# A planner that schedules backward and forward in turn, in a clustered attention with two dense layers

## The chip, the cores and the metric

The kernel runs on one core of a Trainium2 chip. The metric is the device time of one execution in microseconds. The kernel before took 800.88 us (median of three runs, 799.55 to 801.35).

## The reference

Inputs are q, k and v of shape (2, 8, 768, 64), sixteen centroids for each of the 8 heads, and two dense layers with weights 512x2048 and 2048x512 each. A query sees a key only if both have the same nearest centroid:

```python
mask = q_assign[:, :, :, None] == k_assign[:, :, None, :]
scores = np.where(mask, scale * np.matmul(q, k.transpose(0, 1, 3, 2)), -1000000000.0)
attn = softmax(scores)                 # over the keys
x = np.matmul(attn, v)                 # -> (1536, 512), heads side by side
h = x @ w_in;  x = (h * sigmoid(h)) @ w_out
h = x @ w2_in; x = (max(h, 0) + alpha * min(h, 0)) @ w2_out
```

All inputs and the output are float32.

## The kernel before

**Tiles and stages.** The 1536 tokens are 12 tiles of 128. Attention goes in 96 units, one for each tile and head. Every float32 operand is split into a high and a low float16 part, so that a product takes three float16 matmuls (high-high, high-low, low-high).

A unit has a front and a back. `front(u)` runs four matmuls of 384 columns into a score bank (lines 765 and 769; there are two such banks, so two units can be between scores and softmax), a row minimum on VectorE (779), the exponential on ScalarE (784), the high part on ScalarE (791) and the low part on VectorE (793). `front_t(u)` issues one DMA that transposes the unit's probabilities (799). `back(u)` runs eighteen matmuls of 64 columns with v (811); it comes two units behind its front in the program. When the eight heads of a tile are done, line 837 normalizes the tile, and its transposed halves (line 842) are what the first layer reads.

The four weight matrices come in eight pieces each (line 865). A piece is reassembled from its bits on ScalarE (876, 880) and VectorE (887, 890), its sum of squares is taken with eight matmuls (921) and one VectorE instruction (923), and it is split into high and low (902 on ScalarE, 903 on VectorE). The output weights of a layer are split only when all their eight sums are known. `layer1(c)` works through seven chunks of one or two tiles: matmuls of 128 or 256 columns into the w banks (1150), four elementwise instructions (1157, 1158, 1161, 1162), and matmuls with the output weights (1181). `layer2(j)` does the same in three parts of 512 columns (1252, then 1261 to 1266, then 1283). The raw pieces of the second layer's weights lie where attention had its keys and values, so they are loaded from the end of attention on. The sums of squares of the first layer's weights and the chunks' products take the same two w banks in turn, in program order.

**What sets the order.** Each engine and the SP queue of DMAs work in order. The program is first written in one sequence by Python generators (fixed constants say how many units of attention go beside each chunk). At the end `plan_order` hands all instructions to `Plan`, which simulates the engines: `costs` (lines 73 to 107) prices each instruction by its size, `data_deps` (144 to 176) finds which instruction must follow which from the memory cells they touch, and `run(prio)` (178 to 281) is a list scheduler: whenever an engine is free, it takes the ready instruction with the smallest `prio`. The order that comes out is then forced on each engine with order-only dependencies. The priorities are the places in the program:

```python
end, order = plan.run(list(range(len(plan.ins))))
```

Three of its prices are used below. A VectorE instruction of n elements costs 0.145 + n/955 us (0.06 more with a scalar operand from memory), a ScalarE one 0.19 + n/1205 us, and a DMA transposition of n elements per partition lands 1.3 + n/750 + 0.33 us after its issue when the queue is free. In `run`, all DMAs go one behind the other through one `queue`. A PSUM operand is found by `in_psum`, and `cells` gave one cell for each bank of it.

Of the kernel before, what the change touches and what calls it, by code (L numbers as in the profile page):

```python
# [2 lines left out]

# [35 lines left out]
EXP_ON = ("aaaaaaaa", "aaaaaaaa", "aaaaaaaa", "aaaaaaaa")  # L39
P_LO_DVE = range(96)  # L40

MASK = 2.0 ** 15
BIT23 = 2.0 ** 23


class Plan:
# [78 lines left out]
    def cells(self, a):  # L125
        import numpy as np

        b = a.bass_ap
        name = b.tensor.name.rsplit("_", 1)[0]
        if type(b.tensor).__name__.startswith("DRam"):  # L130
            return None, None
        it = 2 if a.dtype in (F16, BF16) else 4
        dims = [list(x) for x in a.ap]
        at = np.array([b.offset % dims[0][0]], dtype=np.int64)
        for st, c in dims[1:]:
            if st:
                at = (at[:, None] + np.arange(c) * st).ravel()
        cell = np.unique(at * it // 4)
        if self.in_psum(a):
            return "ps" + name, np.unique(cell // 512)  # L140
        return name, cell

    def data_deps(self):
# [4 lines left out]
        for n, i in enumerate(self.ins):  # L148
# [26 lines left out]
            found.discard(n)  # L175
            self.deps[n] = sorted(found)

    def run(self, prio):
        import heapq

        N, ne = len(self.ins), len(self.ENGINES)
# [10 lines left out]
        now, later = [[] for _ in range(ne)], [[] for _ in range(ne)]  # L192
        order = [[] for _ in range(ne)]
        queue = end = 0.0
        port = [0.0] * ne
        other = {1: 3, 3: 1}
        window = [0, False, 0.0]
# [4 lines left out]
        for _ in range(N):  # L202
            while True:
                best = None
                for e in range(ne):
                    while later[e] and later[e][0][0] <= free[e]:
                        t, p, n = heapq.heappop(later[e])
# [4 lines left out]
                    t = free[e] if now[e] else later[e][0][0] if later[e] else None  # L212
                    if t is not None and (best is None or t < best[0]):
                        best = (t, e)
                t, e = best
# [3 lines left out]
                p, n = now[e][0]  # L219
# [14 lines left out]
            n = heapq.heappop(now[e])[1]  # L234
            for x in held:
                heapq.heappush(now[e], x)
            s, c = free[e], self.cost[n]
            kind = self.ENGINES[e]
            if kind == "PE":
# [7 lines left out]
                t = c[0] if window[1] else 1.6 * c[0]  # L247
                free[e] = busy[e] = s + t
                done = s + t + 0.23
# [14 lines left out]
            elif kind == "SP":  # L264
# [3 lines left out]
                done = own = queue + 0.33  # L268
                flight.append([done, b, s, n])
            else:  # L270
# [2 lines left out]
                    port[e] = s + c[0] - 0.13  # L273
                done = own = s + c[0] + 0.06
            end = max(end, done)
            order[e].append(n)
            for m, only in after[n]:
                at = s if only else own if self.eng[m] == e else done
# [7 lines left out]
def plan_order(tc, nc, starts):  # L286
    plan = Plan(list(nc.cur_bb.bb.instructions))
    place = {i.name: n for n, i in enumerate(plan.ins)}
    for a, b in starts:
        plan.order_only[place[a]].append(place[b])  # L290
    end, order = plan.run(list(range(len(plan.ins))))
    for line in order:
        for a, b in zip(line, line[1:]):
            tc.add_manual_dep(
                plan.ins[b], plan.ins[a].name,
                mybir.DependencyInfo(mybir.DependencyClass.NoSync, mybir.DependencyReason.DATA),
                reason="planned order",
            )
    return end
# [3 lines left out]
def cluster_attention_silu_prelu(  # L303
# [230 lines left out]
    def one_hot(sims, n, w2, o, a, b, en):  # L534


        y = view(o + KB, F16, n, C)
        z = view(o, F16, n, C)
        m = scr(n)
        nc.vector.reduce_max(out=m, in_=sims, axis=AX.X)  # L540
        nc.vector.tensor_tensor(out=y, in0=sims, in1=bc(m, C), op=ALU.is_equal)
        nc.vector.tensor_tensor(
            out=z, in0=y, in1=rev.unsqueeze(1).to_broadcast([128, n, C]), op=ALU.mult
        )
        m2 = scr(n // 2).bitcast(F16)
        nc.vector.reduce_max(out=m2, in_=z, axis=AX.X)
        nc.vector.tensor_tensor(out=y, in0=z, in1=bc(m2, C), op=ALU.is_equal)
        en.tensor_scalar(w2[:, :, D:D + C], y, a, b, op0=ALU.mult, op1=ALU.add)
# [9 lines left out]
    def k_pre(b, pr):  # L558
        return o_x2 + 6 * KB * pr if b == 0 else o_x2 + (8 + 6 * (pr % 2)) * KB
# [83 lines left out]
    def prep_k_b(b, pr):  # L643
# [4 lines left out]
        for g in range(G):  # L648
            h = 2 * pr + g // T
            for i, c in enumerate((0, 2)):  # L650
# [3 lines left out]
                )  # L654
        one_hot(sims, G, w2, k_pre(b, pr), -MASK, MASK, nc.gpsimd if b or pr else nc.vector)
        k_t2[b, pr] = nc.sync.dma_start_transpose(
# [3 lines left out]
        for j in range(2):  # L660
# [5 lines left out]
        nc.vector.tensor_scalar(  # L666
            has[D:D + C, b, 2 * pr:2 * pr + 2], missing[D:D + C], MASK * (S - 0.5), None,
            op0=ALU.is_lt,
# [38 lines left out]
    def prep_q_b(n):  # L707
# [3 lines left out]
        for h in range(H):  # L711
            for i in range(2):
# [3 lines left out]
                )  # L716
        one_hot(sims, H, w2, o_preq, -MASK, 0.0, nc.gpsimd if n else nc.vector)
        q_t2[n] = nc.sync.dma_start_transpose(
# [4 lines left out]
    def head_scales(n, pairs):  # L723
# [4 lines left out]
        if pairs[0] == 0:  # L728
            (nc.gpsimd if n else nc.vector).tensor_scalar(
                d, isk[b], q_inv[:, n % 2:n % 2 + 1], 1.0 / float(D) ** 0.5 / MASK,  # L730
                op0=ALU.mult, op1=ALU.mult,
# [615 lines left out]
    for j in range(NC2):  # L1347
        layer2(j)
    plan_order(tc, nc, starts)


# [30 lines left out]
```

## Time and profile before

| what | value |
|---|---|
| median of 3 runs | 800.88 us (799.55 to 801.35) |
| the profiled execution | 802.03 us |
| its span, first to last instruction | 800.2 us |
| mean granted TensorE clock | 0.968 of full speed |
| TensorE matmuls busy | 704.5 us, 88% of the span |
| VectorE busy | 539.4 us, 67% |
| ScalarE busy | 450.1 us, 56% |
| GpSimd busy | 144.0 us, 18% |
| DMA queue q1, share of the 16 engines | 59.7% |

PE is TensorE's matmuls, PEld its weight loads (which run beside matmuls), DVE is VectorE, ACT ScalarE, POOL GpSimd, SP the queue that issues all DMAs. A mean over the span says little here, since the kernel goes through stages; the rows below are by stage.

### The profile page before, as it was taken

The page shows a single profiled execution, that of the slowest core. Times are in us where ns is not written, and L with a number is a line of the kernel's source. Part 1 is how long each engine was busy: PE and PEld are TensorE (multiplying, and loading weights), DVE is VectorE, ACT ScalarE, POOL GpSimd, SP SyncE. Part 2 cuts the span into 40 slices and gives each one's busy share as a digit, 9 for nine tenths or more (in the row PEclk, how much of TensorE's full clock was granted, in tenths as well). Part 3 has the DMA queues.
Part 4 walks back from the last instruction along what each step waited for, and adds up shares of the span by engine and source line. Part 5 has one row for each costly group of instructions (what it writes and reads, how often), then busy time and mean ns, then how long its engine had stood idle before and what let it go on. Part 6 is the DMA issues. An engine that isn't in the chain of part 4 may idle for free.

```text
span 800.2 us, 16777 instructions
## 1 busy us (share of the span) xinstructions
PE 704.5 (88%) x6932; PEld 497.1 (62%) x6932; DVE 539.4 (67%) x1024; ACT 450.1 (56%) x725; POOL 144.0 (18%) x237
## 2 busy tenths in 40 slices
PE   1446657779999999999999989999899999999998
PEld 1344445658888887888877879785444444444443
DVE  5589998887678689759867777969940286017700
ACT  7957777777678667758746776866430132012200
POOL 4642131122512643213211030000000000000000
PEclk9996659999999999999999999999999999999999
DMA  9969998879998998997897967630000000000000
GB/s 271 263 169 250 283 279 136 142 152 144 169 171 149 165 173 146 144 171 136 144 130 114 286 172 198 235 135 1 0 1 27 26 1 1 27 26 1 1 27 26
DMA packets 241596, 101.89 MB, mean 127 GB/s; under 512 B 217328, under 2 KB 227568, under 8 KB 241392
## 3 DMA queue, kind: packets, MB, share of 16 engines
q1 hardware_dynamic: 241520, 100.83, 59.7%
q8 instruction: 54, 0.88, 0.5%
q14 instruction: 22, 0.18, 0.1%
HBM read 44.08 MB, written 3.15 MB: 59 GB/s over the span
## 4 chain that ended last, share of the span: by engine, by line
PE 54%; DMA 9%; DVE 5%; issue 3%; ACT 3%; POOL 2%; SPq 0%; POOLq 0%; ACTq 0%
PE w L1283 10%; PE w L1252 9%; PE w L1150 8%; DMA arena<-arena 7%; PE w L1181 7%; PE m L1283 5%; PE m L1252 4%; PE x L811 3%; PE s L765 2%; DMA arena<-in_moe_w_out_dram 2%; PE s L769 1%; DVE arena L903 1%; PE s L921 1%; PE m L1150 1%; DVE arena L890 1%
## 5 line engine op out<-in xcount | busy, mean ns | idle before, releaser
L1181 PE MATMUL w<-arena 128*128 128x256 f16 (+1 forms) x1248 | 132.6, 256 | 5.0 <-ACT arena L1161 2.1
L1150 PE MATMUL w<-arena 128*128 128x256 f16 (+1 forms) x1200 | 127.4, 255 | 2.9 <-DVE arena L1158 1.6
L1181 PEld LDWEIGHTS <-arena 128*128 128x128 f16 x1344 | 114.1, 99 | 18.4 <-DVE arena L903 3.3
L1150 PEld LDWEIGHTS <-arena 128*128 128x128 f16 x1344 | 114.3, 98 | 17.6 <-issue 3.5
L793 DVE TENSOR_TENSOR arena<-arena 128x768 f16<-128x768 f32 x96 | 96.2, 1002 | 26.8 <-ACT arena L791 26.2
L779 DVE TENSOR_SCALAR_CACHE_REDUCE s<-s,stat 128x768 f32<-128x768 f32 x96 | 97.8, 1021 | 16.8 <-PE s L769 10.4
L784 ACT ACTIVATE arena<-s,stat 128x768 f32<-128x768 f32 x96 | 86.0, 896 | 38.8 <-DVE arena L793 26.3
L1252 PEld LDWEIGHTS <-arena 128*128 128x128 f16 x576 | 56.5, 98 | 70.2 <-issue 3.1
L1283 PEld LDWEIGHTS <-arena 128*128 128x128 f16 x576 | 56.3, 98 | 68.0
L791 ACT ACTIVATE arena<-arena 128x768 f16<-128x768 f32 x96 | 80.5, 839 | 24.1 <-DMA arena<-arena 23.7
L1252 PE MATMUL w<-arena 128*128 128x512 f16 x384 | 86.0, 379 | 1.0 <-DVE arena L1262 1.0
L1283 PE MATMUL w<-arena 128*128 128x512 f16 x384 | 83.7, 379 | 0.0
L1261 DVE TENSOR_SCALAR arena<-w,stat 128x512 f32<-128x512 f32 x32 | 23.8, 748 | 88.8 <-PE w L1252 88.8
L1265 ACT ACTIVATE arena<-arena,stat 128x512 f16<-128x512 f32 x48 | 34.3, 720 | 84.2 <-DVE arena L1262 82.3
L765 PE MATMUL s<-arena 80*128 80x384 f16 x192 | 67.9, 354 | 14.7 <-ACT arena L784 9.5
L811 PEld LDWEIGHTS <-arena 128*128 128x128 f16 x1728 | 66.0, 102 | 22.9 <-DMA arena<-arena 17.0
L811 PE MATMUL x<-arena 128*128 128x64 f16 x1728 | 71.3, 199 | 8.9 <-DMA arena<-arena 8.9
L423 POOL TENSOR_SCALAR stat<-stat 128x1 int32<-128x1 int32 x49 | 14.4, 293 | 339.0 <-DVE stat L418 237.3
L769 PE MATMUL s<-arena 128*128 128x384 f16 x192 | 68.2, 355 | 0.0
L1289 ACT ACTIVATE arena<-w,stat 128x512 f32<-128x512 f32 x8 | 5.5, 687 | 73.1 <-PE w L1283 73.1
L903 DVE SCALAR_TENSOR_TENSOR arena<-arena,stat 128x1024 f16<-128x1024 f32 x32 | 41.6, 1311 | 7.1 <-ACT arena L902 7.0
L887 DVE SCALAR_TENSOR_TENSOR arena<-arena 128x1024 int32<-128x1024 int32 x32 | 39.8, 1245 | 9.4 <-ACT arena L880 9.4
(149 smaller groups left out, 1034.1 us busy)
## 6 DMA issues: line engine op xcount, KB each, us to landing
arena<-in_moe_w_in_dram SPq DMA_DIRECT2D x16, 1024.0 KB, 6.2
arena<-in_moe_w_out_dram SPq DMA_DIRECT2D x16, 1024.0 KB, 6.1
arena<-in_k_dram SPq DMA_DIRECT2D x8, 384.0 KB, 4.9
arena<-in_q_dram SPq DMA_DIRECT2D x6, 512.0 KB, 4.5
arena<-in_v_dram SPq DMA_DIRECT2D x8, 384.0 KB, 6.0
out_dram<-arena SPq DMA_DIRECT2D x12, 256.0 KB, 2.0
arena<-arena SPq DMA_TRANSPOSE x149, 4.2
arena<-in_moe_alpha_dram SPq DMA_DIRECT2D x1, 1024.0 KB, 6.6
```

The source lines that it names most:

```text
L765: nc.tensor.matmul(out=sc[:, j, :hs], lhsT=qt2[0:D + C, h], rhs=kt2[0:D + C, h % 2, j * hs:(j + 1) * hs], start=True, stop=False,)
L769: nc.tensor.matmul(out=sc[:, j, :hs], lhsT=qt1[:, h], rhs=kt1[:, h % 2, j * hs:(j + 1) * hs], start=False, stop=True,)
L779: nc.vector.tensor_scalar(sc[:, :, :hs], sc[:, :, :hs], nd_cols[:, H * (n % 2) + h:H * (n % 2) + h + 1], None, op0=ALU.mult, op1=ALU.min, ...
L784: nc.scalar.activation(out=view(o, F32, 2, hs), in_=sc[:, :, :hs], func=ACTF.Exp, scale=-1.0, bias=bias, accum_out=sums[n % 2][:, h:h + 1],)
L791: nc.scalar.activation(out=hl[:, 0], in_=p, func=ACTF.Copy)
L793: en.tensor_tensor(out=hl[:, 1], in0=p, in1=hl[:, 0], op=ALU.subtract)
L811: nc.tensor.matmul(out=x_ps[0][:, h], lhsT=pt[:, ph * T + t], rhs=vt[:, h % 2, t, vh], start=(i == 0), stop=(i == 3 * T - 1),)
L903: nc.vector.scalar_tensor_tensor(out=lo, in0=t, scalar=s, in1=hi, op0=ALU.mult, op1=ALU.subtract)
L1150: nc.tensor.matmul(out=hp[:, ff], lhsT=wi[:, a, kd, ff * 128:ff * 128 + 128], rhs=mov(bb, kd), start=(i == 0), stop=(i == 3 * KD - 1),)
L1181: nc.tensor.matmul(out=acc, lhsT=wo[:, a, f % 2, dt * 128:(dt + 1) * 128], rhs=g[:, f, bb], start=(i == 0), stop=(i == 3 * KF - 1),)
L1252: nc.tensor.matmul(out=hp, lhsT=in_piece(o_a + 24 * KB, f // 2)[:, a, kd, f % 2 * 128:][:, :128], rhs=x[bb][:, kd], start=(i == 0), stop=( ...
L1283: nc.tensor.matmul(out=acc, lhsT=g[:, f, a, t * 128:(t + 1) * 128], rhs=out_piece(o_w, f // 2)[:, bb, f % 2], start=(i == 0), stop=(i == 3 ...
```

## The change

The planner now runs the list scheduler many times. `mirror` makes a copy of the plan with every dependency turned round. `improve` starts with the plan of before (priorities by place in the program). Then sixty times it schedules the mirrored plan with what ended last first, and schedules the real plan again with what ended last in the mirrored one first (those are the instructions with the longest tail of work behind them); a normal noise of 0.1 us is added to the priorities. It keeps the plan with the smallest simulated end, the first one among them. `run` notes when each instruction began and ended. And `cells` gives one cell for a whole PSUM tile: the two halves of a score tile count as one place.

```diff
+PLAN_ROUNDS = 60
...
         if self.in_psum(a):
-            return "ps" + name, np.unique(cell // 512)
+            return "ps" + name, np.zeros(1, np.int64)
         return name, cell
...
+    def mirror(self):
+
+        back = copy(self)
+        back.deps = [[] for _ in self.ins]
+        back.order_only = [[] for _ in self.ins]
+        for n in range(len(self.ins)):
+            for d in self.deps[n]:
+                back.deps[d].append(n)
+            for d in self.order_only[n]:
+                back.order_only[d].append(n)
+        return back
+
+    def improve(self, rounds):
+
+        noise = Random(1)
+        best = self.run(list(range(len(self.ins))))
+        back = self.mirror()
+        for _ in range(rounds):
+            back.run([noise.gauss(0, 0.1) - t for t in self.ended])
+            best = min(best, self.run([noise.gauss(0, 0.1) - t for t in back.ended]), key=lambda x: x[0])
+        return best
+
     def run(self, prio):
...
         queue = end = 0.0
+        self.begun, self.ended = [0.0] * N, [0.0] * N
...
             end = max(end, done)
+            self.begun[n], self.ended[n] = s, done
             order[e].append(n)
...
-    end, order = plan.run(list(range(len(plan.ins))))
+    end, order = plan.improve(PLAN_ROUNDS)
     for line in order:
```

No instruction is added or removed and no buffer is moved; only the order on the five in-order queues can change.

## Rows read from the trace of the kernel before

**Rows 1.** The page, parts 1 and 2: busy time, and tenths in 40 slices of 20 us.

```profile
PE 704.5 (88%) x6932; PEld 497.1 (62%) x6932; DVE 539.4 (67%) x1024; ACT 450.1 (56%) x725; POOL 144.0 (18%) x237
...
PE   1446657779999999999999989999899999999998
...
PEclk9996659999999999999999999999999999999999
```

**Rows 2.** Windows by stage: stretch, length, then busy PE, PEld, DVE, ACT, POOL, clock, DMA, GB/s.

```profile
40.00:123.60 83.60, 50.00 (x519) 36.71 (x516) 78.85 (x163) 58.68 (x80) 23.31 (x34) 0.71 0.97 241
123.60:180.00 56.40, 43.58 (x712) 36.25 (x712) 47.10 (x90) 42.64 (x76) 11.89 (x21) 0.97 0.79 142
180.00:440.00 260.00, 251.56 (x3463) 214.52 (x3462) 197.96 (x405) 180.96 (x330) 75.99 (x102) 1.00 0.91 150
440.00:543.00 103.00, 95.83 (x964) 84.66 (x963) 79.98 (x133) 75.02 (x104) 9.72 (x22) 1.00 0.67 200
543.00:600.00 57.00, 54.26 (x257) 25.06 (x255) 46.25 (x67) 26.63 (x40) 0.34 (x2) 1.00 0.00 1
```

**Rows 3.** Timeline, TensorE (last row ScalarE): start, length, instruction, [idle before].

```profile
123.62 0.27 PE L1150 MATMUL w<-arena 128*128 128x128 f16 x2 [1.12 <-DVE arena L923]
123.73 0.33 PE L765 MATMUL s<-arena 80*128 80x384 f16 x1
...
124.23 0.33 PE L769 MATMUL s<-arena 128*128 128x384 f16 x1
...
478.03 5.95 PE L1181 MATMUL w<-arena 128*128 128x256 f16 x53
...
542.95 0.38 PE L1252 MATMUL m<-arena 128*128 128x512 f16 x1
...
796.49 0.69 ACT L1289 ACTIVATE arena<-w,stat 128x512 f32<-128x512 f32 x1 [9.67 <-PE w L1283]
```

**Rows 4.** Groups of VectorE instructions from 40 to 123.6 us: count | busy, mean ns.

```profile
L887 DVE SCALAR_TENSOR_TENSOR arena<-arena 128x1024 int32<-128x1024 int32 x13 | 16.6, 1276 | 0.0
L890 DVE SCALAR_TENSOR_TENSOR arena<-arena 128x1024 int32<-128x1024 int32 x13 | 16.4, 1260 | 0.0
L779 DVE TENSOR_SCALAR_CACHE_REDUCE s<-s,stat 128x768 f32<-128x768 f32 x16 | 16.2, 1021 | 0.7 <-PE s L769 0.7
L793 DVE TENSOR_TENSOR arena<-arena 128x768 f16<-128x768 f32 x13 | 12.3, 949 | 0.2 <-ACT arena L791 0.2
...
L779 DVE DVE_READ_ACCUMULATOR s<-s,stat 128x1 f32 x16 | 2.2, 136 | 0.0
```

**Rows 5.** Timeline of VectorE: the last splits of weights, the first and last tile's end.

```profile
93.13 1.28 DVE L903 SCALAR_TENSOR_TENSOR arena<-arena,stat 128x1024 f16<-128x1024 f32 x1
...
103.24 0.68 DVE L837 TENSOR_TENSOR arena<-x,stat 128x512 f32<-128x512 f32 x1
...
165.47 2.48 DVE L903 SCALAR_TENSOR_TENSOR arena<-arena,stat 128x1024 f16<-128x1024 f32 x2
...
475.05 0.69 DVE L837 TENSOR_TENSOR arena<-x,stat 128x512 f32<-128x512 f32 x1
```

**Rows 6.** Waits of TensorE from 123.6 to 180 us: total, times, longest.

```profile
PE s L765 <- ACT arena L784: 5.0, 4, 1.7
PE x L811 <- DMA arena<-arena: 2.9, 5, 0.9
...
PE w L1181 <- DVE arena L903: 1.8, 5, 0.7
```

**Rows 7.** The page, part 5: groups over the whole span.

```profile
L1181 PEld LDWEIGHTS <-arena 128*128 128x128 f16 x1344 | 114.1, 99 | 18.4 <-DVE arena L903 3.3
...
L793 DVE TENSOR_TENSOR arena<-arena 128x768 f16<-128x768 f32 x96 | 96.2, 1002 | 26.8 <-ACT arena L791 26.2
...
L791 ACT ACTIVATE arena<-arena 128x768 f16<-128x768 f32 x96 | 80.5, 839 | 24.1 <-DMA arena<-arena 23.7
...
L903 DVE SCALAR_TENSOR_TENSOR arena<-arena,stat 128x1024 f16<-128x1024 f32 x32 | 41.6, 1311 | 7.1 <-ACT arena L902 7.0
```

**Rows 8.** The 96 transpositions of line 799, in ns, and their landing.

```profile
L799 SPq EVENT_SEMAPHORE  x128: 17/28/4110, 39.8 to 464.6; - x128
L799 SPq DMA_TRANSPOSE arena<-arena x96: 1274/1442/5193, 45.4 to 465.0; - x96
...
DMA to landing us min/median/max: 3.6/4.2/9.0
```

**Rows 9.** Waits over the whole span: total us, times, longest.

```profile
PE x L811 <- DMA arena<-arena: 8.9, 16, 1.3
```

More of the change, by code (lines that the diff above doesn't have):

```diff
@@ L2 @@
 from contextlib import ExitStack
+from copy import copy
+from random import Random
 import concourse.bass as bass
```

## The prediction

> **What bounds the kernel now.** I read the page's busy rows first: TensorE is the busiest engine with 704.5 of 800.2 us, and in the 40 slices it is full from the ninth or tenth slice on, while the slices before show tenths of 1 to 7 and, from 60 to 120 us, a granted clock of 0.5 to 0.6, which is mostly the lower of its two levels (1.2 of 2.4 GHz) [rows 1]. So a new order can only win where TensorE has holes, and the second thing to read is a cut of the span at the events that close a stage.
>
> The timeline of TensorE gives the cuts. The first product of the first layer starts at 123.62 us, released by line 923; the second layer starts at 542.95 us; the last eviction begins at 796.49 us, when TensorE is done [rows 3]. Windows between these cuts give TensorE's holes [rows 2]: 83.6 - 50.0 = 33.6 us from 40 to 123.6 us, 56.4 - 43.58 = 12.8 us up to 180, 260 - 251.56 = 8.4 us up to 440, 103 - 95.83 = 7.2 us up to the second layer, 2.7 us in its first 57 us. Behind that TensorE has none, so the 200 us from 600 us on cannot be shortened by any order.
>
> In the first of these windows TensorE is not the bound. VectorE is busy 78.85 of 83.6 us there, 94% [rows 2]. What it does is two sorts of work mixed: pieces of weights (lines 887 and 890 thirteen times each, 33.0 us) and attention (line 779 sixteen times, 793 thirteen times, with the accumulator reads 16.2 + 12.3 + 2.2 = 30.7 us) [rows 4]. The first product needs tile 0, which is eight units; it ended at 103.24 us [rows 5]. The other eight of the sixteen units are tile 1, which the first chunk does not need.
>
> **The change, part by part.** *The sixty rounds.* They add no instruction. What they can alter is which ready instruction an engine takes. The new priority is the length of the tail behind an instruction; weights of the first layer have nearly the whole kernel behind them, tile 1's attention has less. So I expect VectorE and ScalarE to do pieces of weights first and tile 1 later. What that is worth at most: eight times line 779 with its read, 8 x (1.021 + 0.136) = 9.3 us, and five of line 793 beyond tile 0's eight, 5 x 0.949 = 4.7 us, 14.0 us of a full VectorE ahead of 123.62 us [rows 4]. Not all is won: TensorE must then run these eight fronts later, when it is full. Four score matmuls start at intervals of (124.23 - 123.73) / 3 = 0.167 us, so a front is 0.67 us and eight are 5.3 us [rows 3]. Net 14.0 - 5.3 = 8.7 us; since tile 0 itself still has to pass through tile normalization at 103.24 us and its transposition, I take 8. The bounds are 0 and 14.
>
> The moved work lands on VectorE between 180 and 440 us, which has 260 - 197.96 = 62 us free there [rows 2]: that covers the 14 us. If that cover were gone, the same 14 us would come back as holes before 440 us.
>
> *From 123.6 to 180 us*, holes of 12.8 us. TensorE waits 5.0 us for a score bank held by the exponential, 2.9 us for transposed probabilities, 1.8 us for splits of the output weights, which end only at 165.47 + 2.48 us [rows 5, 6]. These splits have a long tail behind them and will be taken earlier; the other two waits can be filled with products if these are ready. Bounds 0 and 12.8, I take half, 6.
>
> *From 180 to 440 us*, holes of 8.4 us, many and small; bounds 0 and 8.4, I take 2. Here a rule of the Trainium skill would say otherwise, so the row comes first. A row of 53 products of 256 columns lasts 5.95 us, and by the 0.27 us that one or two take, the interval is about (5.95 - 0.27) / 52 = 0.109 us [rows 3]; 256 columns at 2.4 GHz would be 0.107. A busy TensorE is thus at its rate here and its holes are all that can be won. The Trainium skill (Perfetto Trace Analysis, Identifying the Most-Contended Engine) says that busy matmul time is a poor measure of the distance to the limit, and that the busy share of weight loads is a good one. By that rule this stretch would have 260 - 214.52 = 45.5 us of room [rows 2], and with a quarter of it the term would be 11 us, not 2. The interval of the products speaks against it, and I stay with the holes.
>
> *From 440 to 600 us*, holes of 7.2 + 2.7 = 9.9 us. VectorE is busy 79.98 of 103 and 46.25 of 57 us there [rows 2], converting the second layer's weights behind the end of attention at 475.05 us [rows 5]. Bounds 0 and 9.9, I take 4.
>
> *The SP queue and the DMAs* are reordered too. A transposition that waits for its unit at the head of the queue holds all DMAs behind it; the waits on line 799 have a median of 0.028 us and a largest of 4.1 us [rows 8]. The change could spare or add such waits; between -4 and +4 us I take 0 and leave the rest to a rival. GpSimd's queue is busy 18% [rows 1]; a step that moves on it has idle time to hide in.
>
> *One cell for a PSUM tile* joins the two halves of a score tile in one chain of four matmuls. Line 779 reads both halves anyway, and the four run in a row in 0.67 us [rows 3]; I cost it at nothing, covered by that. Without the cover it could hold a second half back by one front, 0.67 us now and then.
>
> *Sum.* 8 + 6 + 2 + 4 = 20 us. The profiled execution took 802.0 us, so 782.0 us; it lay 1.15 us above the median of 800.88 us, so **781 us**. A measurement of this kernel can tell about 0.2% from no change.
>
> **Can the planner's prices be trusted?** This decides whether a plan that is shorter in the planner is shorter on the chip. For line 793 it has 0.145 + 768/955 = 0.949 us, the row has 1.002; for line 903 0.145 + 1024/955 + 0.06 = 1.277 against 1.311; for line 791 0.19 + 768/1205 = 0.827 against 0.839 [rows 7]. These are low by 1 to 6%. For a transposition of 1536 elements it has 1.3 + 2.05 + 0.33 = 3.68 us from issue to landing, the row has a median of 4.2 and up to 9.0 [rows 8]. That one is low by 0.52 us.
>
> **The rivals.** *Slower: backs wait for their transpositions.* A scheduler that ranks by tails packs a back (line 811) right behind the moment at which it believes the probabilities have landed. TensorE works in order, so if they come 0.52 us later, every product behind the back waits too. If this hits half of the 96 units, it is 48 x 0.52 = 25 us, 5 more than the gain, and the time is 806 us. It decides against the change from 20 / 96 = 0.21 us per unit on. For it: the low price and the scatter of the landing [rows 8]. Against it: the plan of before has the same price, and there TensorE waits for transpositions in 16 places, 8.9 us together [rows 9].
>
> *Nothing changes.* The first plan stays in the comparison; if none of the sixty is shorter in the planner, the order is that of before, but for the cells. Also the gain at the start may be hidden: the two w banks force sums and products into program order, so that the start at 123.62 us waits for line 923 of the output weights anyway [rows 3]. Time 799 to 802 us. Against it: 14 us of work that nobody needs yet, on a VectorE that is 94% busy, is what a ranking by tails finds.
>
> *Much more is won.* If all upper bounds come together, 14 + 12.8 + 8.4 + 9.9 = 45 us, the time is 756 us. Three quarters of it, 34 us, give 767 us. For it: sixty plans are a wide search, and the low clock from 60 to 120 us would go sooner with denser work. Against it: VectorE and ScalarE carry 47.1 and 42.64 us of the 56.4 after 123.6 us [rows 2], and lines 784 to 793 with the transposition are a chain that only two score banks overlap.
>
> **How the numbers follow.** The forecast (a gain of about 6 to 31 us, 770 to 795 us) has 0.50, much more won 0.20, nothing changed 0.10, slower 0.20. So faster by over 0.2% is 0.70, within 0.2% is 0.10, slower is 0.20. For 8 in 10 I leave out half of the case of much more (below 762 us) and half of the slower one (above 806 us): 762 to 806 us. The unknown costs, the +4 or -4 us of the SP queue and the bounds of the four terms, lie inside.
>
> **What would show it.** Right: the first product of line 1150 starts near 115 us, not 123.6; the last split of the output weights ends before 160 us; fewer than eight units of tile 1 stand ahead of the first product; the second layer starts near 523 us. Wrong: line 811 waits for transpositions longer than 8.9 us in total; the first product is no earlier, being still behind line 923; the end of attention moves past 475 us and the holes before the second layer grow beyond 7.2 us. If TensorE's order is the same as before, the planner kept its first plan.

## The result and the profile after

The kernel after takes **791.30 us** (median of 4 runs, 790.88 to 791.85) against 800.89 us before: a ratio of 0.9883, 95% interval 0.9866 to 0.9900. It is faster, as forecast, and inside the range of 762 to 806 us, but the gain is 9.6 us where 20 were forecast. The profiled execution took 791.62 us, its span is 789.9 us, 10.3 less than before.

All line numbers behind `improve` are 27 higher than before: 1150 is 1177, 811 is 838, 837 is 864, 903 is 930, 1252 is 1279.

The page of the kernel after, parts 1 and 2, beside [rows 1]:

```profile
PE 709.3 (90%) x6932; PEld 501.3 (63%) x6932; DVE 541.1 (69%) x1024; ACT 450.1 (57%) x725; POOL 143.4 (18%) x237
...
PE   1365669789999999999999999999999999999998
...
PEclk9996559889999999999999999999999999999999
```

The instructions are as many as before on every engine. TensorE's row has lost its eights in the middle (slices 23 and 28 of before) and is full from the tenth slice on. The span is 10.3 us shorter although TensorE's busy time grew by 709.3 - 704.5 = 4.8 us; its idle time fell from 95.7 to 80.6 us.

The same five windows as in [rows 2]:

```profile
40.00:123.60 83.60, 54.53 (x564) 40.02 (x563) 80.17 (x168) 62.26 (x84) 24.26 (x34) 0.69 1.02 249
123.60:180.00 56.40, 48.55 (x759) 40.90 (x757) 50.53 (x94) 43.48 (x80) 15.11 (x22) 0.91 0.92 162
180.00:440.00 260.00, 252.12 (x3425) 214.40 (x3422) 200.60 (x405) 183.13 (x329) 71.18 (x101) 1.00 0.89 155
440.00:543.00 103.00, 98.91 (x945) 84.99 (x944) 80.63 (x136) 76.09 (x104) 10.14 (x24) 0.98 0.57 176
543.00:600.00 57.00, 57.00 (x266) 25.82 (x264) 39.15 (x56) 20.56 (x33) 0.00 (x0) 1.00 0.01 5
```

TensorE's holes shrink in all five, least where most of the time is: from 8.4 to 7.9 us in 180 to 440 us. In the last row they are gone (2.7 before). But VectorE in the first row, which was to be relieved, is busier than before (80.17 against 78.85 us).

The events that close the stages, on the timelines of TensorE and ScalarE, beside [rows 3]:

```profile
117.65 1.64 PE L1177 MATMUL w<-arena 128*128 128x128 f16 x22
...
535.08 0.59 PE L1279 MATMUL m<-arena 128*128 128x512 f16 x1
...
786.12 0.69 ACT L1316 ACTIVATE arena<-w,stat 128x512 f32<-128x512 f32 x1 [9.46 <-PE w L1310]
```

And on VectorE's, beside [rows 5]: the ends of tiles 0, 3, 10 and 11 (line 864) and the last split of the first layer's output weights (930):

```profile
108.08 0.68 DVE L864 TENSOR_TENSOR arena<-x,stat 128x512 f32<-128x512 f32 x1
...
166.27 1.28 DVE L930 SCALAR_TENSOR_TENSOR arena<-arena,stat 128x1024 f16<-128x1024 f32 x1
...
204.22 0.69 DVE L864 TENSOR_TENSOR arena<-x,stat 128x512 f32<-128x512 f32 x1 [2.32 <-PE x L838]
...
427.31 0.68 DVE L864 TENSOR_TENSOR arena<-x,stat 128x512 f32<-128x512 f32 x1
...
467.09 0.69 DVE L864 TENSOR_TENSOR arena<-x,stat 128x512 f32<-128x512 f32 x1 [0.43 <-PE x L838]
```

Tiles 3 and 10 in the kernel before, VectorE's timeline:

```profile
208.16 0.69 DVE L837 TENSOR_TENSOR arena<-x,stat 128x512 f32<-128x512 f32 x1 [1.31 <-PE x L811]
...
433.70 0.69 DVE L837 TENSOR_TENSOR arena<-x,stat 128x512 f32<-128x512 f32 x1 [0.57 <-issue]
```

The lead of after over before, read from event to event, shows where the time comes from:

| event | before | after | lead, us |
|---|---|---|---|
| end of tile 0 | 103.24 | 108.08 | -4.8 |
| first product of layer 1 | 123.62 | 117.65 | 6.0 |
| end of tile 3 | 208.16 | 204.22 | 3.9 |
| end of tile 10 | 433.70 | 427.31 | 6.4 |
| end of tile 11 | 475.05 | 467.09 | 8.0 |
| first product of layer 2 | 542.95 | 535.08 | 7.9 |
| last eviction begins | 796.49 | 786.12 | 10.4 |

So 6.0 us come at the first product, 2 of them are lost again up to tile 3, 4 come back up to the end of attention, and 2.5 come in the second layer, where the holes are gone. These are readings of one execution each: two programs with the same order (before and e1_cells_only, below) differ at the same events by up to 1.1 us. The last split ends at 167.55 us; before it was 167.95. It has not moved.

### The profile page after: what moved, and what is told of

Read it like the earlier page. It is cut to its first block, busy times and chain, and to the rows that moved or that the text cites. A ratio compares the mean times of both kernels' runs of the same rounds, so it can differ in the third digit from the quotient of the medians.

```text
span 789.9 us, 16751 instructions
## 1 busy us (share of the span) xinstructions
PE 709.3 (90%) x6932; PEld 501.3 (63%) x6932; DVE 541.1 (69%) x1024; ACT 450.1 (57%) x725; POOL 143.4 (18%) x237
## 3 DMA queue, kind: packets, MB, share of 16 engines
HBM read 44.08 MB, written 3.15 MB: 60 GB/s over the span
## 4 chain that ended last, share of the span: by engine, by line
PE 55%; DMA 12%; ACT 5%; DVE 5%; issue 4%; POOL 2%; POOLq 0%; SPq 0%; ACTq 0%; DVEq 0%
PE w L1279 11%; PE w L1310 10%; DMA arena<-arena 9%; PE w L1208 8%; PE w L1177 6%; PE m L1279 5%; PE m L1310 5%; PE x L838 3%; PE s L792 2%; PE s L796 2%; DMA arena<-in_moe_w_out_dram 1%; DVE arena L820 1%; PE s L948 1%; ACT arena L818 1%; DMA arena<-in_moe_w_in_dram 1%
## 5 line engine op out<-in xcount | busy, mean ns | idle before, releaser
L1208 PE MATMUL w<-arena 128*128 128x256 f16 (+1 forms) x1248 | 140.8, 257 | 3.3 <-DVE arena L930 3.0
L1177 PE MATMUL w<-arena 128*128 128x256 f16 (+1 forms) x1200 | 132.0, 257 | 1.1 <-DVE arena L1185 0.9
L1208 PEld LDWEIGHTS <-arena 128*128 128x128 f16 x1344 | 114.1, 99 | 17.8 <-DVE arena L930 3.8
L1177 PEld LDWEIGHTS <-arena 128*128 128x128 f16 x1344 | 114.9, 99 | 16.0 <-issue 2.2
L1279 PEld LDWEIGHTS <-arena 128*128 128x128 f16 x576 | 56.8, 99 | 68.3 <-issue 2.1
L1310 PEld LDWEIGHTS <-arena 128*128 128x128 f16 x576 | 56.4, 98 | 68.0
L1279 PE MATMUL w<-arena 128*128 128x512 f16 x384 | 93.0, 381 | 0.0
L838 PE MATMUL x<-arena 128*128 128x64 f16 x1728 | 77.7, 199 | 13.4 <-DMA arena<-arena 13.4
L1310 PE MATMUL w<-arena 128*128 128x512 f16 x384 | 85.7, 379 | 0.0
L838 PEld LDWEIGHTS <-arena 128*128 128x128 f16 x1728 | 70.5, 102 | 23.3 <-DMA arena<-arena 19.4
L450 POOL TENSOR_SCALAR stat<-stat 128x1 int32<-128x1 int32 x49 | 20.7, 424 | 336.5 <-DVE stat L445 231.5
L1279 PE MATMUL m<-arena 128*128 128x512 f16 x192 | 50.5, 383 | 0.0
L914 DVE SCALAR_TENSOR_TENSOR arena<-arena 128x1024 int32<-128x1024 int32 x32 | 40.8, 1277 | 12.6 <-ACT arena L907 12.6
```

Of the source, the lines that this page charges most:

```text
L838: nc.tensor.matmul(out=x_ps[0][:, h], lhsT=pt[:, ph * T + t], rhs=vt[:, h % 2, t, vh], start=(i == 0), stop=(i == 3 * T - 1),)
L914: nc.vector.scalar_tensor_tensor(out=lo, in0=hi, scalar=3, in1=lo, op0=ALU.logical_shift_left, op1=ALU.bitwise_or)
L1177: nc.tensor.matmul(out=hp[:, ff], lhsT=wi[:, a, kd, ff * 128:ff * 128 + 128], rhs=mov(bb, kd), start=(i == 0), stop=(i == 3 * KD - 1),)
L1208: nc.tensor.matmul(out=acc, lhsT=wo[:, a, f % 2, dt * 128:(dt + 1) * 128], rhs=g[:, f, bb], start=(i == 0), stop=(i == 3 * KF - 1),)
L1279: nc.tensor.matmul(out=hp, lhsT=in_piece(o_a + 24 * KB, f // 2)[:, a, kd, f % 2 * 128:][:, :128], rhs=x[bb][:, kd], start=(i == 0), stop=( ...
L1310: nc.tensor.matmul(out=acc, lhsT=g[:, f, a, t * 128:(t + 1) * 128], rhs=out_piece(o_w, f // 2)[:, bb, f % 2], start=(i == 0), stop=(i == 3 ...
```

## The experiments

The kernel computes its plan itself, so each version has a number of the planner's own: the simulated end. It is not a time of the chip, but it can be held against one. "Plan" is that end less the 777.1 of the kernel before (the plan of e4_landing is its order at the price that the others have), "chip" the ratio to the kernel before with its 95% interval, and "chip, us" what that ratio makes of 800.9 us. The other columns are read from the timelines as above.

| kernel | plan, us | chip | chip, us | first product | last split ends | tile 11 |
|---|---|---|---|---|---|---|
| before | 0 | 1 | 0 | 123.6 | 168.0 | 475.1 |
| after, 60 rounds | -12.1 | 0.9883 [0.9866, 0.9900] | -9.4 | 117.7 | 167.6 | 467.1 |
| e1_cells_only | 0 | 0.9999 [0.9979, 1.0020] | -0.1 | 123.5 | 168.6 | 474.1 |
| e3_worst | +1.5 | 1.0084 [1.0057, 1.0111] | +6.7 | 117.8 | 163.2 | 479.0 |
| e7_300_rounds | -12.6 | 0.9872 [0.9836, 0.9909] | -10.3 | 119.4 | 168.9 | 466.8 |
| e5_no_or | -11.9 | 0.9910 [0.9879, 0.9941] | -7.2 | 122.4 | 171.5 | 467.3 |
| e6_half_loads | -19.3 | 0.9779 [0.9751, 0.9807] | -17.7 | 118.2 | 169.3 | 457.9 |
| e8_tile1_later | -9.0 | 0.9912 [0.9883, 0.9942] | -7.0 | 125.4 | 170.4 | 471.0 |
| e4_landing | +4.2 | 0.9973 [0.9952, 0.9993] | -2.2 | 121.4 | 168.8 | 473.6 |
| e11_early | +3.5 | 0.9966 [0.9946, 0.9986] | -2.7 | 118.7 | 167.1 | 468.0 |
| e12_late | -6.4 | 0.9936 [0.9911, 0.9960] | -5.1 | 123.7 | 169.9 | 471.7 |
| e9_constants | -18.3 | 0.9682 [0.9662, 0.9703] | -25.5 | 117.8 | 166.4 | 458.4 |
| e10_constants | -18.6 | 0.9748 [0.9725, 0.9772] | -20.2 | 121.1 | 167.4 | 463.6 |
| e13_constants_0 | +11.3 | 1.0130 [1.0100, 1.0160] | +10.4 | 121.5 | 167.2 | 476.6 |

### The cells alone

```diff
-PLAN_ROUNDS = 60
+PLAN_ROUNDS = 0
```

> The merged cell of a PSUM tile alone, with no rounds of improvement: the planner's end is 777.1 with it as without. Both theories: the order of the kernel before, 799 to 803 us. If it differs by over 3 us, part of the change's effect belongs to the cells.

Measured: 801.87 us against 801.49, no difference. The order of the instructions is that of before on all five engines, one by one, so joining the two halves of a score tile does nothing in the plan in program order. What the cells do to the sixty plans was not tried by itself.

This pair also tells how far a window's busy time can be read. The same two windows of before and of e1_cells_only, two programs with the same order:

```profile
40.00:117.65 77.65, 45.76 (x481) 33.64 (x477) 72.93 (x153) 55.62 (x73) 23.31 (x34) 0.72 0.96 241
117.65:180.00 62.35, 47.81 (x750) 39.32 (x751) 53.03 (x101) 45.69 (x83) 11.89 (x21) 0.94 0.83 152
```

```profile
40.00:117.65 77.65, 47.77 (x480) 34.48 (x476) 72.94 (x153) 55.70 (x74) 24.03 (x34) 0.85 0.97 241
117.65:180.00 62.35, 51.62 (x761) 43.31 (x762) 53.97 (x104) 45.76 (x84) 12.56 (x21) 0.86 0.84 154
```

The granted clock differs (0.72 against 0.85, then 0.94 against 0.86), TensorE's busy time differs by 2.0 and 3.8 us, and the span is 799.7 against 800.2 us. So in these two windows a few us of "holes" come and go with no change of order and none of the time. From 180 to 535 us, where the clock is 1.00 in both, TensorE's rows agree within 0.3 us.

### The longest of the sixty plans

```diff
-            best = min(best, self.run([noise.gauss(0, 0.1) - t for t in back.ended]), key=lambda x: x[0])
+            best = max(best, self.run([noise.gauss(0, 0.1) - t for t in back.ended]), key=lambda x: x[0])
```

> The planner keeps the longest of its sixty plans instead of the shortest. By the planner's own ends the plan of before is 777.1, the kept one 765.0, this one 778.6. Theory (the chip follows the planner, at about 0.8 to 0.9 of a difference): 800 to 804 us, no faster than the kernel before. Rival (a ranking by tails helps as such, and which of the sixty is kept is luck): 790 to 796 us, like the changed kernel.

Measured: 808.96 us against 802.08, slower. Its first product, last split and last tile on the timelines of TensorE and VectorE, and two of its windows (same columns as before):

```profile
117.79 1.39 PE L1177 MATMUL w<-arena 128*128 128x128 f16 x22
...
161.92 1.27 DVE L930 SCALAR_TENSOR_TENSOR arena<-arena,stat 128x1024 f16<-128x1024 f32 x1
...
479.00 0.69 DVE L864 TENSOR_TENSOR arena<-x,stat 128x512 f32<-128x512 f32 x1 [0.82 <-PE x L838]
```

```profile
180.00:440.00 260.00, 246.25 (x3310) 207.99 (x3307) 197.70 (x393) 177.94 (x321) 72.30 (x103) 0.99 0.87 147
440.00:535.00 95.00, 88.72 (x889) 78.21 (x887) 74.19 (x119) 67.15 (x90) 8.30 (x19) 0.96 0.73 203
```

This is also a plan ranked by tails. Its first product is as early as in after (117.79 against 117.65 us) and its splits end 4.4 us earlier; yet it is slower by some 16 us. It loses them later: 13.75 us of holes from 180 to 440 us against 7.9 in after. An early first product and early splits are therefore not enough by themselves, and a ranking by tails alone is not the gain, since this plan has it too: choosing among the plans is.

### More rounds

```diff
-PLAN_ROUNDS = 60
+PLAN_ROUNDS = 300
```

> The changed kernel with 300 rounds instead of sixty, the base of the two edits. The planner's end goes from 765.0 to 764.5. Theory (the search is at its floor after sixty rounds, the floor is set by resources and not by the order): 789.5 to 792.5 us. Rival (the gain fell short because sixty plans are too few): 780 to 787 us.

Measured: 792.79 us against 802.08. The intervals of sixty and three hundred rounds overlap; the search is at its floor. The next four kernels have 300 rounds too and are held against this one; the first two ran beside it.

### VectorE relieved

```diff
-        nc.vector.scalar_tensor_tensor(
-            out=lo, in0=hi, scalar=3, in1=lo, op0=ALU.logical_shift_left, op1=ALU.bitwise_or
-        )
+        if w2:
+            nc.vector.scalar_tensor_tensor(
+                out=lo, in0=hi, scalar=3, in1=lo, op0=ALU.logical_shift_left, op1=ALU.bitwise_or
+            )
```

> Leaves out the first of the two bit operations on each of the sixteen pieces of the first layer's weights: 16 VectorE instructions of 1.27 us, 20 us, all before the first layer's last sum; 300 rounds of planning. Theory A (VectorE bounds the time up to the end of the first layer's splits, as the prediction had it): the first product 8 or more us earlier than 117.65 us, 778 to 785 us. Theory B (the DMA queue, the loads and transpositions of the first 110 us, bounds it; VectorE only looks full): within 2 us of the same planning without this edit, 789 to 792 us.

Measured: 794.73 us, where e7_300_rounds took 792.79 beside it. The first window of e7_300_rounds, then that of e5_no_or, and the latter's first product on TensorE's timeline:

```profile
40.00:117.65 77.65, 47.75 (x472) 35.62 (x471) 74.07 (x158) 58.66 (x77) 22.91 (x34) 0.71 1.02 257
```

```profile
40.00:117.65 77.65, 48.02 (x492) 35.47 (x491) 62.43 (x146) 57.35 (x75) 19.98 (x33) 0.71 0.97 256
```

```profile
122.41 1.11 PE L1178 MATMUL w<-arena 128*128 128x128 f16 x17
```

VectorE has 11.6 us less to do in that window (20 us over all sixteen pieces), and nothing comes earlier: the first product not, tile 0 not (108.6 against 108.4 us), the end not. A VectorE that is busy 74.07 of 77.65 us was not what the stage waited for. Among what stayed as it was are the last two columns, the DMAs' share of about 1 and 256 GB/s.

### Half the bytes of the first layer's weights

```diff
+        a = w.shape[0] // 128
+        m = a if w2 else a // 2
         return nc.sync.dma_start(
-            out=raw.rearrange("p (a f) c -> p a (f c)", a=w.shape[0] // 128),
-            in_=w.bitcast(I32).rearrange("(a p) f -> p a f", p=128),
+            out=raw.rearrange("p (a f) c -> p a (f c)", a=a)[:, :m],
+            in_=w.bitcast(I32).rearrange("(a p) f -> p a f", p=128)[:, :m],
         )
```

> Loads only half of each piece of the first layer's weights (the other half of the buffer is set to zero once, four GpSimd instructions of about 0.9 us), and works on the rest as before: 8.4 MB less through the DMA queue in the first 110 us, the same work on all engines; 300 rounds of planning. Theory A (VectorE is the bound): within 2 us of the same planning without the edit, 789 to 792 us. Theory B (the DMA queue is): 781 to 786 us, the first product 5 or more us earlier.

Measured: 784.57 us, 8.2 less than e7_300_rounds. Two windows of e6_half_loads, the ends of its tiles 0 and 11 on VectorE's timeline, and the landing of its transpositions (line 826) from 40 to 118 us. The weights have 8 bytes an element (not float32, as the section on the reference says of all inputs), so this edit spares 8.4 MB (the page has 35.69 MB read from memory in place of 44.08):

```profile
40.00:117.65 77.65, 51.32 (x555) 39.42 (x555) 74.11 (x149) 61.49 (x86) 23.71 (x35) 0.70 0.82 178
180.00:440.00 260.00, 256.01 (x3466) 220.60 (x3465) 204.11 (x416) 185.32 (x334) 71.84 (x103) 1.00 0.92 162
```

```profile
98.19 0.68 DVE L864 TENSOR_TENSOR arena<-x,stat 128x512 f32<-128x512 f32 x1
...
457.93 0.69 DVE L864 TENSOR_TENSOR arena<-x,stat 128x512 f32<-128x512 f32 x1
```

```profile
DMA to landing us min/median/max: 3.6/3.9/6.4
```

The same landing in e7_300_rounds:

```profile
DMA to landing us min/median/max: 3.8/4.5/8.0
```

With 178 GB/s in place of 257 tile 0 ends 10.2 us earlier than in e7_300_rounds (98.19 against 108.43) and tile 11 8.9 us earlier (457.93 against 466.78), with VectorE as busy as it was (74.11 us). The transpositions land in 3.9 instead of 4.5 us, which is too little for that by itself. A part of the lead is there before the window: the first row minimum starts at 37.63 us against 41.38, and in the first 40 us VectorE has done 26.90 us of work against 19.88. The lead is in attention alone: the first product stays at 118.2 us (119.4 in e7_300_rounds) and the last split at 169.3. It pays all the same, since TensorE then finds more to do between 180 and 440 us (256.01 busy against 252.16 in e7_300_rounds). Of the two that were relieved in the first stage, VectorE and the DMA queue, it is the DMA queue that counts for the end of the kernel, with the order searched anew for each. For the first product neither counts for much: it comes 3.0 us later in e5_no_or and 1.2 us earlier here.

### Tile 1 behind a weight piece

```diff
+    for u in range(8, 16):
+        starts.append((fronts[u].ins.name, last_bits[15].ins.name))
     plan_order(tc, nc, starts)
```

> Forces what the prediction thought the ranking would do: line 806 of units 8 to 15 (tile 1) may not start before the last piece of the first layer's weights has had its first bit operation; 300 rounds of planning. Theory of the prediction (VectorE's 14 us for tile 1 ahead of the first product are free to be moved): the first product and the splits of the output weights 8 us earlier, 780 to 787 us. Rival (the first stage is bound by the DMA queue and by tile 0's own chain, and the moved work is missed later by TensorE): the splits come earlier, but the last tile's end comes later than the 467 us of the plans without this order, 794 to 799 us.

Measured: 795.51 us, where e7_300_rounds took 792.79; the intervals of the two ratios overlap, so it is not faster, and not clearly slower. The first product and the end of tile 0 of e8_tile1_later on the timelines, and its first window:

```profile
125.41 2.59 PE L1179 MATMUL w<-arena 128*128 128x128 f16 x39
...
114.84 0.69 DVE L866 TENSOR_TENSOR arena<-x,stat 128x512 f32<-128x512 f32 x1 [1.16 <-PE x L840]
```

```profile
40.00:117.65 77.65, 44.15 (x427) 32.75 (x426) 69.50 (x144) 54.49 (x69) 22.72 (x33) 0.91 0.93 237
```

The edit ties tile 1 to the piece of weights that is last in the program, and the search went round it. It took that piece fifteenth and let another one be last. VectorE's timeline, with the first bit operation (line 916) of the fifteenth and the sixteenth piece and the first row minimum (808) of tile 1:

```profile
104.35 1.22 DVE L916 SCALAR_TENSOR_TENSOR arena<-arena 128x1024 int32<-128x1024 int32 x1
105.48 1.02 DVE L808 TENSOR_SCALAR_CACHE_REDUCE s<-s,stat 128x768 f32<-128x768 f32 x1
...
119.12 1.22 DVE L916 SCALAR_TENSOR_TENSOR arena<-arena 128x1024 int32<-128x1024 int32 x1
```

Five units of tile 1 start between the two pieces, and fourteen of the sixteen units stand ahead of the first product, as in after. So tile 1 was held back for a while and not moved behind the first product, and what all of the prediction's 14 us would have been worth was not run. What did move brought nothing: the first product is 6.0 us later than in e7_300_rounds, and VectorE did not use the room, being busy 69.50 us in place of 74.07.

### Transpositions priced as they land

```diff
-                done = own = queue + 0.33
+                done = own = queue + (0.85 if c[0] > 1 else 0.33)
```

> The planner believes that every transposition lands 0.52 us later than it did (the measured median instead of its price); 300 rounds. The prediction's rival (backs packed behind a landing that is priced too low cost time): line 838 waits for transpositions less than the 13.4 us of the changed kernel, and 785 to 789 us. Other theory (the waits are set by loads in front of the transpositions, which no constant meets): 790 to 795 us, the waits on transpositions still 10 us or more.

Measured: 800.61 us against 801.49, a gain of 2.2 us where e7_300_rounds, which differs from it in this price alone, gains 10.3. TensorE's waits for transpositions (line 838) and for the exponential (811) in after, in e7_300_rounds and in e4_landing (total, times, longest):

```profile
PE x L838 <- DMA arena<-arena: 13.4, 19, 1.8
...
PE s L792 <- ACT arena L811: 5.5, 6, 2.4
```

```profile
PE s L792 <- ACT arena L811: 11.5, 11, 1.9
...
PE x L838 <- DMA arena<-arena: 5.2, 9, 0.9
```

```profile
PE s L792 <- ACT arena L811: 10.5, 10, 2.4
...
PE x L838 <- DMA arena<-arena: 1.8, 4, 0.8
```

After has 4.5 us more of the waits for transpositions than before [rows 9], as the slower rival had it. But e7_300_rounds, at the same price, has only 5.2 us of them and is no faster than after: their total does not go with the time. With the higher price they fall from 5.2 to 1.8 us, the waits for the exponential stay about where they were (11.5 and 10.5 us), and the kernel loses some 8 us of the gain. What it loses is in the order itself, which in the planner, at the old price, ends 16.7 us later than that of e7_300_rounds. Nor does this price make the planner a better judge: at it, the order of after would end at the same 780.5 us as that of e4_landing, and on the chip after is faster by some 7 us. Whether another price, nearer to the landing in each stage, would win was not tried.

### The two halves of the order

Line numbers in these two are 31 higher than before. `t0` are the starts in program order, `t1` those of the best plan.

```diff
-        return best
+        return self.run([t1[n] if t1[n] < 180 else 1e4 + n for n in place])
```

> The improved order for what the improved plan begins in its first 180 us, and behind that the ready instruction with the smallest place in the program, as before. Theory 1 (the gain is made in the first stages and only has to be kept): 790 to 794 us. Theory 2 (the planner's view: 780.6 for this plan against 777.1 before and 765.0 for the whole one; without the later order the head start is lost again): 800 to 806 us.

```diff
-        return best
+        return self.run([t0[n] - 1e4 if t0[n] < 180 else t1[n] for n in place])
```

> The other half: the order of before for what the first plan begins in its first 180 us, the improved one behind it. Theory 1 (the gain is made in the first stages): 799 to 802 us. Theory 2 (the planner's view, 770.7): 794 to 798 us.

Measured: 799.85 and 797.30 us against 803.11. The early half gives 0.34%, 2.7 us, the late half 0.64%, 5.1 us; together 7.8 of the 9.4. The early half is instructive by its milestones: first product 118.7 and last tile 468.0 us, nearly those of after, and yet most of that lead is gone at the end (span 798.2 against 789.9). Here a lead paid only with the order behind it that was made for it.

### Other constants

The fixed constants of the program (how many units run beside each chunk, when weights, keys and values are loaded, which engine scales k and v) were chosen again, by the shortest end after planning. For e9_constants the main ones are as follows (the order of the v loads, the engines of four scalings and some steps of the weights' work changed too):

```diff
-UNITS_FIRST = 17
-UNITS_BY_CHUNK = (32, 53, 64, 69, 98, 98, 98)
+UNITS_FIRST = 18
+UNITS_BY_CHUNK = (31, 53, 60, 69, 96, 98, 98)
-W_LOAD_AT = (0, 1, 3, 5)
+W_LOAD_AT = (0, 1, 3, 4)
-Q_AT = (0, 4)
+Q_AT = (1, 4)
-PLAN_ROUNDS = 60
+PLAN_ROUNDS = 300
```

> The changed kernel with 300 rounds and other constants, found by letting the planner rank many of them: one unit more ahead of the first chunk, three key scalings and one value scaling moved between ScalarE and GpSimd, one query step and one weight load issued at another unit, some weight tasks moved by a unit. The planner's end is 758.8 against 764.5. Theory (the chip follows the planner): 784 to 788 us. Rival (below some 765 the planner's differences are noise): 790 to 795 us.

e10_constants is another set, found in the same way, with 300 rounds and, among other changes,

```diff
-UNITS_BY_CHUNK = (32, 53, 64, 69, 98, 98, 98)
+UNITS_BY_CHUNK = (32, 53, 70, 74, 94, 98, 98)
-W1_OUT_AT = 16
+W1_OUT_AT = 12
-W_LOAD_AT = (0, 1, 3, 5)
+W_LOAD_AT = (0, 1, 3, 3)
```

> Another such set, found from another start (some units more beside the chunks 2 and 3, the output weights' scale four steps earlier, a few low parts of probabilities on GpSimd). The planner's end is 758.5. Theory (the chip follows the planner): 784 to 788 us. Rival (noise): 790 to 795 us.

Measured: 777.25 and 782.75 us against 803.11; both beat both kernels. Two windows of e9_constants:

```profile
180.00:440.00 260.00, 255.89 (x3439) 219.56 (x3438) 202.75 (x410) 187.50 (x337) 70.46 (x100) 1.00 0.91 160
440.00:535.00 95.00, 95.00 (x900) 79.37 (x898) 77.03 (x122) 66.76 (x88) 13.26 (x20) 1.00 0.60 176
```

From 440 to 535 us there is no hole left (7.2 before, 4.1 in after), and from 180 to 440 us 4.1 us. The last run takes these constants with the plan in program order (not that of a backward plan, as its expectation has it):

```diff
-PLAN_ROUNDS = 300
+PLAN_ROUNDS = 0
```

> The constants of e9_constants, but with no plan of the sixty: the units are issued in the order of the first backward plan, as in the kernel before. The plan's own end is 788.4 us, against 777.1 with the old constants in that order and 758.8 with these constants and 300 rounds. Theory (the chip follows the plan's end, and these constants pay only together with an order that was searched for them): the kernel before's 801 plus 788.4 less 777.1, so about 812, 806 to 818. Rival (what e9_constants won lies in the constants themselves, by fewer conflicts of the loads and helpers whatever the order): 785 to 795.

Measured: 811.14 us against 801.60. Its window from 535 us on and the longest wait in it, for an elementwise step of the second layer (line 1286, 1262 in the kernel before), which ends at 577.90 us:

```profile
535.00:600.00 65.00, 53.47 (x293) 26.42 (x292) 60.23 (x95) 37.73 (x55) 1.12 (x4) 0.92 0.19 65
```

```profile
PE w L1276 <- DVE arena L1286: 8.5, 2, 8.3
```

The rival falls: without the search these constants cost 10 us, with it they win 25. What the rounds are worth thus depends on the program that they start from: 9 us with the old constants, some 34 to 36 with these.

## Why the prediction was right or wrong

**Right: what decides.** A shorter plan in the planner is a faster kernel on the chip, within limits. Of the twelve kernels in the table whose plan differs from that of before, ten have the same sign in plan and chip. The two others, e4_landing and e11_early, have plans some 4 us longer and came out 2 to 3 us faster; so plans that differ by a few us can come out either way. The rival that nothing changes fell, and so did "much more": 300 rounds add nothing, and the granted clock from 40 to 123.6 us, which that rival counted on, is 0.69 in place of 0.71.

**Right, by these milestones: the last two terms.** The holes of the second layer are gone and the lead grows by 2.5 us there; with the 1.5 between tile 10 and layer 2 the fourth term gave 4.0, as forecast. The third, 180 to 440 us, was forecast as 2; the lead grows by 2.5 from tile 3 to tile 10.

**Wrong: the first two terms, 8 and 6 us.** The first product came 6.0 us earlier in place of 8. The step from 123.6 to 180 us, which was to add 6, gave no lead: at tile 3 it is 3.9 us, 2.0 less. These two miss the forecast by 2 + 8 = 10 us, about all of the difference between 20 and the 10.3 of the span. Of the four signs for "right" one came: six units of tile 1 ahead of the first product in place of eight. The first product is at 117.65 us, not near 115, the last split at 167.55, not before 160, and the second layer at 535.08, not near 523.

The step that failed is the reading of the first window, "VectorE is busy 78.85 of 83.6 us there", as the bound, and "These splits have a long tail behind them and will be taken earlier". Of the sixteen units ahead of the first product, fourteen are still there. VectorE's groups from 40 to 117.65 us, in after, beside [rows 4]:

```profile
L806 DVE TENSOR_SCALAR_CACHE_REDUCE s<-s,stat 128x768 f32<-128x768 f32 x14 | 14.1, 1018 | 0.1
L820 DVE TENSOR_TENSOR arena<-arena 128x768 f16<-128x768 f32 x11 | 10.6, 964 | 0.6 <-ACT arena L818 0.6
```

Two instructions of each sort moved behind the first product, about 4 us, not 14. And the runs show that there was less to win here than the busy share said: relieving VectorE by 20 us moves nothing (e5_no_or), holding tile 1 back for a while does not help (e8_tile1_later), halving the loads moves attention by 9 to 10 us (e6_half_loads). The DMA share of 0.97 and 241 GB/s stood in the first row of [rows 2]; the prediction cited the row for TensorE and VectorE and did not weigh that column. As for the splits, the sums that they need were done 8 us earlier (line 950 at 122.43 us, 923 at 130.42 before) and the first split began 10 us earlier (145.82 against 155.54), but the last one ended at 167.55 us as before, and TensorE's waits for them from 123.6 to 180 us grew from 1.8 to 3.0 us. Nor do early splits pay alone: in e3_worst they end 4.4 us earlier, in a slower kernel.

A further step put every us of hole at a us of time. From 123.6 to 180 us the holes did shrink, from 12.8 to 7.9 us, and the waits for the exponential from 5.0 to 0.7, and yet no lead came of it. In the whole span TensorE's idle time fell by 15.1 us and the span by 10.3. Holes are no room by themselves: with the order of before, e1_cells_only has 799.7 - 710.9 = 88.8 us of idle time, 6.9 less than before, and a span only 0.5 us shorter; 3.8 of the 6.9 lie from 117.65 to 180 us, at a clock of 0.86 in place of 0.94.

**The slower rival** had its mechanism half right: waits for transpositions did grow in after, from 8.9 to 13.4 us, a sign that the prediction had named for "wrong". They did not turn the sign, and e7_300_rounds is as fast with 5.2 us of them. So they are no measure of the time, and e4_landing shows that pricing them away, at least with this price, costs more than they do.

**What stays open.** What sets the first product's time: neither VectorE nor the loads moved it below 117.6 us. It is not tile 0 alone: in e6_half_loads tile 0's transposed halves (line 869) land at 101.7 + 3.3 = 105.0 us, in after at 113.1 + 3.1 = 116.2, and the first product comes at 118.2 and 117.7. What the prediction's 14 us of tile 1 would be worth if they were all moved. And why e9_constants gains 25 us for a plan that is 18 shorter.

## What to carry to other kernels

A stage in which one engine is 94% busy may still wait for another queue: read the DMA share and the rate of the same row, and relieve each suspect once before pricing a gain by the busiest. When an order is searched, it is the choice of the shortest plan that pays and not the ranking rule alone, a lead at one milestone is worth little unless the order behind it uses it, and constants that were tuned for the old order should be tuned again with the search inside the loop: that gave 15 us more here than the search with the old ones. And when an experiment ties an instruction down in a searched order, look in the trace whether the search kept to what was meant.

## What was not expected of the hardware

Two programs with the same order on every engine ran from 40 to 117.65 us at a granted clock of 0.72 and 0.85 and started the first product at 123.62 and 123.48 us (before and e1_cells_only). In both TensorE stood idle ahead of it, for 1.12 and 0.98 us, until line 923 (950) of VectorE was done. So the lower clock cost nothing at this milestone.

How long a transposition takes to land differs by stage, and within a stage from order to order. The medians of line 799 (826) from 40 to 118 us, over 10 to 15 transpositions each, are, at 241 to 257 GB/s, 6.4 us in before, 5.4 in after, 4.5 in e7_300_rounds and 4.2 in e5_no_or; in e6_half_loads, at 178 GB/s, it is 3.9. The rate of the stretch alone does not set it, then. The landing in the kernel before from 40 to 118 us, and from 180 to 440 us, at 150 GB/s:

```profile
DMA to landing us min/median/max: 3.6/6.4/6.9
```

```profile
DMA to landing us min/median/max: 3.6/4.2/6.2
```

So the 4.2 us of the whole span, with which the prediction reckoned, is a median over stages that differ.
